# The first u spectra of an FFT convolution made ahead of and between the rounds of K's transform

## The chip, the cores and the metric

The kernel runs on one core of a Trainium2 chip. The metric is the device time of one launch in microseconds (us), the median of several runs. A core has TensorE (PE, with its weight loads shown apart as PEld), VectorE (DVE), ScalarE (ACT), GpSimd (POOL) and SyncE (SP), which here only issues DMAs. Each engine takes its own instructions in program order; semaphores order them against each other. TensorE writes to PSUM, which has eight banks of 2 KB per partition; SBUF holds everything else on the chip.

## The reference, cut to what matters

The block is an adaptive layer norm around a state space convolution (part A), and then around a spatial mixer with an MLP (part B). The change lies in part A.

```python
def _A_ref(u, A_re, A_im, B_re, B_im, C_re, C_im, log_dt, Dskip):
    ...
    P = jnp.exp(logdA[:, :, None] * l[None, None, :])
    K = jnp.einsum("dn,dnl,dn->dl", Cc, P, dB).real
    ...
    Kf = rfft2(Kp[:, None, :])
    Uf = rfft2(up[:, :, None, :])
    Yf = Uf * Kf[None, :, :, :]
    y = irfft2(Yf, s=(1, L2))[:, :, 0, :L]
    y = y.transpose(0, 2, 1) + u * Dskip[None, None, :]
    return y
...
h = _layernorm(x) * (1 + ca) + sa
x = x + ga * _A_ref(h, ...)
h = _layernorm(x) * (1 + cb) + sb
x = x + gb * _B_ref(h, ...)
```

u has 2048 rows of 512 channels, and N is 128. The convolution is made by products of transforms over 4096 points.

## The kernel before, in words

All of it is straight-line code, and the order of the instructions on every engine is that of the Python text (`manual_schedule`).

**The chunks** (L510 to L536). K is made in 32 chunks. Chunk k makes sines and cosines (`turns`), their products with exponentials on VectorE (`products`), and a burst of 64 matmuls into PSUM (`burst`, L485). A list `side[k]` adds to some chunks the normalising of u and u's first transform, whose results (`vs`) go out to the DRAM scratch VU (L437). The last of these stores belong to chunk 30. Each block of VU that is read later takes rows from all 64 columns that these stores write. Behind the chunks K gets its skip term (L536), and the first half of the table T2 is loaded (L538).

**K's first transform** (`k_first`, L559). Eight rounds r. A round issues 8 x 4 matmuls (L565; the chip runs each in two instructions, 64 a round) of 32 rows by 128 columns over 64 moving columns, into four PSUM banks, named by BANK as pk1, pk2, pz and py, each of which exists twice: eight banks. Then the four banks are copied to VK, two by ACT and two by DVE (L567 to L571; ACT's copies show as L118, the helper's line).

**The spectra loop** (L899). Sixteen steps, n = 0 to 15, one for each pair (jh, kc). `spectrum_u` (L589) makes u's spectrum of a step from a block of VU and T2, into pk1, and ACT copies it to us; `spectrum_k` (L612) makes K's from VK, T2 and T3 into both buffers of pk2; `multiply` (L623 to L628) is eight operations of DVE that read pk2 and us and write zc; `back` (L638) transforms zc of the step before into pz, ACT copies it to z, and POOL stores z to the DRAM scratch ZT (L641). Before the loop come the eight rounds and the u spectrum of step 0; step n makes the u spectrum of step n + 1. T2's second half (L915) is needed from kc = 4 on. In steps 11 to 13 the first inverse transforms (`inverse`, L663) are made from blocks of ZT.

**Loads.** SP issues them in the order of the text. Blocks of VU (`load_vu`, L578, two DMAs of 256 KB), of ZT (`load_inv`, L647) and raw weights (L676) share one pool, ldp, of seven buffers of 4 KB per partition. A load waits until its buffer's last reader is done, and SP's later loads queue behind it.

**After the loop** the remaining inverse transforms are made, and then part B runs: a mixer (`mix_w`) whose result goes through DRAM (GD), and the MLP (`chan`). A pool hv holds its windows: win, wh and wl, one buffer each.

## Time and profile before

| what | us |
|---|---|
| median of 3 runs | 823.54 (819.7 to 824.34) |
| the profiled execution | 824.95 |
| its span, first to last instruction | 823.2 |
| PE, PEld, DVE, ACT, POOL busy | 721.7, 547.0, 511.0, 339.1, 93.1 |
| chunks, about | 55 to 261 |
| `k_first` | 261.6 to 292.3 |
| spectra loop, to the last inverse transform in front of the mixer's load wait | 292.4 to 395.4 |
| the rest | 395.4 to 823.2 |

How to read it. A profile is of one execution. A timeline row gives start, length, engine, line, operation, out<-in, rows*columns of the array for a matmul, the shape, how many instructions are merged into the row, and in brackets how long the engine was idle before it and what released it. SPq is SP's queue of DMA issues. A line of grouped instructions ends with busy us, mean ns of one, and idle us in front of them by releaser. The row PEclk has one digit for each fortieth of the span: the TensorE clock granted, in tenths of full speed. "issue" is time in which an engine waited for nothing that the profile shows.

### The profile page before, as it was taken

Reading aid. Unit: us, or ns where it says so; the run is one execution under the profiler, and the core shown is the slowest. Engines: PE = TensorE matmul, PEld = TensorE weight load, DVE = VectorE, ACT = ScalarE, POOL = GpSimd, SP = SyncE. Lnnn points to the kernel's source line nnn. Section 1 sums busy time; section 2 is a strip of 40 time slices with the busy share of each in tenths; the row PEclk is TensorE's granted clock in tenths of the full one; section 3 lists DMA queues with packets and bytes.
Section 4 is the critical chain, followed back from the end, with each engine's and each line's share of the span. In section 5 each row is a group of like instructions: output and inputs, shape, how many; then the busy total and the mean of one; then the engine's idle time right before and its main releaser. Section 6 shows DMA issues by size and latency. Waiting matters only on the chain. (4 is left out here: it accounts for less than half of the span.)

```text
span 823.2 us, 17182 instructions
## 1 busy us (share of the span) xinstructions
PE 721.7 (88%) x7256; PEld 547.0 (66%) x7256; DVE 511.0 (62%) x883; ACT 339.1 (41%) x540; POOL 93.1 (11%) x186
## 2 busy tenths in 40 slices
PE   3597888988987989999549888999999999999994
PEld 1254455655556965665238887888888888888883
DVE  8779389988776347686479996644436261715211
ACT  3575467867674334454125553222213121221220
POOL 1011011111000000000126331010101010101000
PEclk9797788978788589999769899999999999999997
DMA  8231514242226999495703554110101010101011
GB/s 295 93 104 52 135 32 98 48 104 53 47 44 160 246 216 300 155 298 191 263 31 92 187 168 123 28 33 20 52 1 52 1 52 1 26 1 26 1 26 25
DMA packets 51045, 79.86 MB, mean 97 GB/s; under 512 B 5172, under 2 KB 37816, under 8 KB 49432
## 3 DMA queue, kind: packets, MB, share of 16 engines
q1 hardware_dynamic: 44808, 57.92, 25.9%
q0 software_dynamic: 6160, 20.85, 7.9%
q8 instruction: 57, 0.93, 0.5%
q14 instruction: 20, 0.16, 0.1%
HBM read 52.53 MB, written 26.21 MB: 96 GB/s over the span
## 5 line engine op out<-in xcount | busy, mean ns | idle before, releaser
L851 DVE TENSOR_TENSOR gl<-gf,gh 128x512 fp32r<-128x512 f32 (+1 forms) x48 | 30.4, 644 | 150.2 <-ACT gh L118 150.2
L118 ACT ACTIVATE gf<-pm 128x512 f32<-128x512 f32 (+1 forms) x48 | 27.0, 563 | 181.7 <-PE pm L845 178.1
L845 PE MATMUL pm<-nh,w3l 128*128 128x256 f32 (+1 forms) x352 | 98.5, 280 | 0.0
L844 PE MATMUL pm<-nl,w3h 128*128 128x256 f32 (+1 forms) x352 | 98.5, 280 | 0.0
L843 PE MATMUL pm<-nh,w3h 128*128 128x256 f32 (+1 forms) x352 | 98.4, 279 | 0.0
L856 PE MATMUL pa<-w4h,gh 128*128 128x512 f32 (+1 forms) x176 | 73.8, 419 | 3.2 <-ACT gh L118 0.9
L857 PE MATMUL pa<-w4l,gh 128*128 128x512 f32 (+1 forms) x176 | 69.3, 394 | 0.0
L843 PEld LDWEIGHTS pm<-nh,w3h 128*128 128x128 f32 (+1 forms) x352 | 65.4, 186 | 1.8
L845 PEld LDWEIGHTS pm<-nh,w3l 128*128 128x128 f32 (+1 forms) x352 | 65.5, 186 | 1.2
L844 PEld LDWEIGHTS pm<-nl,w3h 128*128 128x128 f32 (+1 forms) x352 | 65.2, 185 | 0.6
L858 PE MATMUL pa<-w4h,gl 128*128 128x512 f32 (+1 forms) x176 | 64.1, 395 | 0.0
L471 DVE SCALAR_TENSOR_TENSOR e<-sn,p 128x512 f32<-128x512 f32 x64 | 41.2, 685 | 26.1 <-PE kp L485 18.5
L451 PE MATMUL xx<-MG,ON 64*128 64x512 f32 x160 | 56.5, 454 | 0.0
L452 PE MATMUL xx<-MG,ON 64*128 64x512 f32 x160 | 56.5, 454 | 0.0
L118 ACT ACTIVATE sn<-xx 128x1024 f32<-128x1024 f32 x32 | 32.9, 1029 | 31.2 <-issue 17.7
L864 POOL DMA_DIRECT2D out<-KX x32 | 16.1, 508 | 257.1 <-DVE KX L862 257.1
L750 PE MATMUL pm<-nl,w1h 128*128 128x256 f32 x128 | 39.0, 305 | 6.8 <-DVE nl L721 6.8
L856 PEld LDWEIGHTS pa<-w4h,gh 128*128 128x128 f32 (+1 forms) x176 | 33.0, 188 | 17.8 <-ACT gh L118 13.2
L451 PEld LDWEIGHTS xx<-MG,ON 64*128 64x128 f32 x160 | 36.6, 228 | 7.7 <-issue 0.8
L485 PEld LDWEIGHTS kp<-e,e 128*32 128x32 f32 x2048 | 31.0, 112 | 15.6 <-issue 6.9
L473 DVE TENSOR_TENSOR e<-cs,p 128x1024 f32<-128x1024 f32 x32 | 39.0, 1218 | 1.5 <-ACT cs L118 1.5
L749 PE MATMUL pm<-nh,w1h 128*128 128x256 f32 x128 | 39.2, 306 | 0.0
(215 smaller groups left out, 1899.2 us busy)
## 6 DMA issues: line engine op xcount, KB each, us to landing
VU<-vs SPq DMA_DIRECT2D x64, 128.0 KB, 2.4
ld<-VU SPq DMA_DIRECT2D x32, 256.0 KB, 6.8
ZT<-z POOLq DMA_DIRECT2D x16, 512.0 KB, 4.2
ld<-ZT SPq DMA_DIRECT2D x16, 512.0 KB, 5.6
xu<-in_wm SPq DMA_DIRECT2D x6, 1024.0 KB, 9.9
wst<-in_w SPq DMA_DIRECT2D x18, 256.0 KB, 4.7
xu<-in_u SPq DMA_DIRECT2D x16, 256.0 KB, 4.2
KX<-in_u SPq DMA_DIRECT2D x16, 256.0 KB, 8.4
```

The lines of the kernel that those rows point to most:

```text
L118: return S.activation(out, in_, f, bias=bias, scale=scale)
L451: T.matmul(x[:, :512], la, ma, start=(i == 0), stop=(i == len(ops) - 1))
L452: T.matmul(x[:, 512:], lb, mb, start=(i == 0), stop=(i == len(ops) - 1))
L471: V.scalar_tensor_tensor(e0[:, 1, a], sn[:, 0], 1.0 - 2.0 * a, mg[:, a], op0=OP.mult, op1=OP.mult)
L473: V.tensor_mul(e0[:, 0], cs[:, 0:1].to_broadcast([128, 2, 512]), mg)
L749: T.matmul(p[:, e], W1h[:, k, c], hi[k], start=(k == 0), stop=False)
L843: T.matmul(p[:m, e], W3h[:, k, c], hi[k], start=(k == 0), stop=False)
L844: T.matmul(p[:m, e], W3h[:, k, c], lo[k], start=False, stop=False)
L845: T.matmul(p[:m, e], W3l[:, k, c], hi[k], start=False, stop=(k == 3))
L856: T.matmul(acc[i], gh[:m, e, s], W4h[:m, f], start=(f == 0), stop=False)
L857: T.matmul(acc[i], gh[:m, e, s], W4l[:m, f], start=False, stop=False)
L858: T.matmul(acc[i], gl[:m, e, s], W4h[:m, f], start=False, stop=(f == 10))
```

## The change

It does six things. T2's first half is loaded in chunk 25, and the blocks of u for steps 0, 1 and 2 in chunk 31, into a new pool lda of three buffers that lives from the chunks to the end. All blocks of VU now go through lda. The u spectrum of step 0 is made ahead of round 0, those of steps 1 and 2 behind rounds 1 and 4; step n (1 to 13) makes that of step n + 2, and us has three buffers. `k_first` no longer uses pk1: its rounds go in turn over pk2, pz and py, twice each, so six banks; DVE takes a third copy in rounds 1, 2, 4 and 5. ldp has four buffers, and some of the later loads (one ZT pair of each half, the second matrix's raw weights) go to lda. The pool hv is gone: the windows, wh and wl of part B take buffers of lda.

```diff
@@ -396,6 +396,7 @@
         V.tensor_mul(mods[0], mods[0], mods[2])
     pr.close()
 
+    lda = ctx.enter_context(pool("lda", bufs=3, side="right", reuse_waits="tile"))
     wk = a1.enter_context(pool("wk", bufs=2, reuse_waits="tile"))
     wk1 = a1.enter_context(pool("wk1", bufs=1, reuse_waits="tile"))
     uv = a1.enter_context(pool("uv", bufs=2, reuse_waits="tile"))
@@ -489,6 +490,15 @@
             g0 = (k // 2) * 8
             later.append(lambda: act(Kq[:, g0 // 64, g0 % 64:g0 % 64 + 8], kp))
 
+    vus = {}
+    steps = [(jh, kc) for jh in range(2) for kc in range(8)]
+
+    def load_vu(jh, kc):
+        t = vus[jh, kc] = lda.tile([128, 4, 256], F32, name="ld")
+        for ri in range(2):
+            Y.dma_start(t[ri * 64:ri * 64 + 64],
+                        dram(VU, jh * 1048576 + (ri * 32 + kc * 4) * 16384, [[256, 64], [16384, 4], [1, 256]]))
+
 
     side = {k: [] for k in range(40)}
     for n in range(3, 6):
@@ -505,6 +515,16 @@
             side[at(i) + 2].append(lambda i=i: u_dft(i - 1, 1))
         if i % 4 == 3 and i < 8:
             side[at(i) + 2].append(lambda i=i: load_u(i // 4 + 2))
+
+    T2 = []
+
+    def load_t2(i):
+        T2.append(up.tile([128, 16, 128], F32, name="xu"))
+        Y.dma_start(T2[i], A["T2"].rearrange("p (a b) -> p a b", a=32)[:, i * 16:i * 16 + 16])
+
+    side[25].append(lambda: load_t2(0))
+    for i in range(3):
+        side[31].append(lambda i=i: load_vu(*steps[i]))
 
     later = []
     with tc.manual_schedule():
@@ -534,9 +554,6 @@
         for f in later:
             f()
         V.tensor_add(Kq[:, :, :, 31], DS.rearrange("p (h g) -> p h g", h=2), Kq[:, :, :, 31])
-        T2 = [up.tile([128, 16, 128], F32, name="xu") for i in range(2)]
-        load_t2 = lambda i: Y.dma_start(T2[i], A["T2"].rearrange("p (a b) -> p a b", a=32)[:, i * 16:i * 16 + 16])
-        load_t2(0)
     a1.close()
 
 
@@ -548,16 +565,17 @@
     FI = c2.tile([128, 16, 2, 64], F32, name="FI")
     VK = [v0x.enter_context(pool("v0", side="right")).tile([128, 64, 2, 64], F32, name="VK0"),
           c2.tile([128, 64, 2, 64], F32, name="VK1")]
-    ldp = a2.enter_context(pool("ldp", bufs=7))
+    ldp = a2.enter_context(pool("ldp", bufs=4))
     s2x = ExitStack()
     s2 = s2x.enter_context(pool("s2", bufs=2))
     psy = a2.enter_context(pool("psy", bufs=2, space=PSUM, side="right"))
     psa = s2x.enter_context(pool("psa", bufs=2, space=PSUM))
-    BANK = ("pk1", "pk2", "pz", "py")
-    block = lambda: ldp.tile([128, 4, 256], F32, name="ld")
+    BANK = ("pk2", "pz", "py")
+    block = lambda pl: pl.tile([128, 4, 256], F32, name="ld")
 
     def k_first(r):
-        ps = [(psy if n == "py" else psa).tile([128, 8, 64], F32, name=n) for n in BANK]
+        ps = [(psy if n == "py" else psa).tile([128, 8, 64], F32, name=n)
+              for n in (BANK[(r * 4 + j) % 3] for j in range(4))]
         kv = KX.rearrange("p (g x) -> p g x", g=64)
         for gl in range(8):
             for j in range(4):
@@ -565,22 +583,16 @@
                 T.matmul(ps[j][:, gl], kv[rows, r * 8 + gl], FK[rows], start=True, stop=True)
         for j in range(4):
             o, i = VK[j // 2][:, :, j % 2, r * 8:r * 8 + 8], ps[j].rearrange("p g x -> p x g")
-            if j % 2:
+            if j % 2 or j == 2 and r in (1, 2, 4, 5):
                 V.tensor_copy(o, i)
             else:
                 act(o, i)
 
-    vus, zis, zcs = {}, {}, {}
-
-    def load_vu(jh, kc):
-        t = vus[jh, kc] = block()
-        for ri in range(2):
-            Y.dma_start(t[ri * 64:ri * 64 + 64],
-                        dram(VU, jh * 1048576 + (ri * 32 + kc * 4) * 16384, [[256, 64], [16384, 4], [1, 256]]))
+    zis, zcs = {}, {}
 
     def spectrum_u(jh, kc):
         vu = vus.pop((jh, kc))
-        us = s2.tile([128, 2, 3, 256], F32, name="us")
+        us = s2.tile([128, 2, 3, 256], F32, name="us", bufs=3)
         for i in range(2):
             q = psa.tile([128, 2, 256], F32, name="pk1")
             for ro in range(2):
@@ -641,7 +653,7 @@
         P.dma_start(ZT[jh][:, kc * 4:kc * 4 + 4], z)
 
     def load_inv(jh, g):
-        zz = [block() for h in range(2)]
+        zz = [block(lda if (jh, g) in ((0, 2), (1, 0)) else ldp) for h in range(2)]
         for h in range(2):
             c0 = 12 - 4 * g if h == 0 else 4 * g
             Y.dma_start(zz[h], dram(ZT[jh], (h * 16 + c0) * 32768, [[256, 128], [32768, 4], [1, 256]]))
@@ -683,8 +695,8 @@
             return split
         return hi, lo, load
 
-    def two(m, n):
-        return block().rearrange("p (a c) b -> p a (c b)", a=2)
+    def two(pl):
+        return lambda m, n: block(pl).rearrange("p (a c) b -> p a (c b)", a=2)
 
     def rstd(r, v):
         n = r.shape[-1]
@@ -756,7 +768,7 @@
         if g not in (0, 7):
             return
         if hf == 0:
-            win["pd"] = hv.tile([128, 4, 256], F32, name="win")
+            win["pd"] = block(lda)
         pd = win["pd"][:, hf * 2:hf * 2 + 2]
         gv = go.rearrange("p f (s c) -> p (f s) c", s=2)
         pv = pd.rearrange("p f (s c) -> p (f s) c", s=2)
@@ -773,14 +785,14 @@
     cn = {}
 
     def chan_load(g):
-        w = win[g] = hv.tile([128, 4, 256], F32, name="win")
+        w = win[g] = block(lda)
         for f, sh in enumerate((-1, 1, -2, 2)):
             Y.dma_start(w[:, f], dram(GD, f * 128 * 2560 + (2 + 2 * g + sh) * 128, [[2560, 128], [1, 256]]))
 
     def chan_split(g):
         w = win[g]
-        wh = hv.tile([128, 4, 256], F32R, name="wh")
-        wl = hv.tile([128, 4, 256], F32R, name="wl")
+        wh = lda.tile([128, 4, 256], F32R, name="ld")
+        wl = lda.tile([128, 4, 256], F32R, name="ld")
         act(wh, w)
         V.tensor_sub(wl, w, wh.bitcast(F32))
         win[g] = wh, wl
@@ -882,23 +894,21 @@
 
     seq = (7, 0, 1, 2, 3, 4, 5, 6)
 
-    steps = [(jh, kc) for jh in range(2) for kc in range(8)]
     with tc.manual_schedule():
         t3 = A["T3"].rearrange("p (a b) -> p a b", a=32)
-        load_vu(*steps[0])
         Y.dma_start(T3[:, :16], t3[:, :16])
         Y.dma_start(Gm, A["G"].rearrange("p (a b) -> p a b", a=2))
+        us = [spectrum_u(*steps[0])]
+        load_vu(*steps[3])
         for r in range(8):
             k_first(r)
-            if r == 3:
-                load_vu(*steps[1])
-            if r == 6:
-                load_vu(*steps[2])
-        us = spectrum_u(*steps[0])
+            if r in (1, 4):
+                us.append(spectrum_u(*steps[len(us)]))
+                load_vu(*steps[len(us) + 2])
         split = None
         for n, st in enumerate(steps):
             p = spectrum_k(*st)
-            multiply(*st, us, p)
+            multiply(*st, us[n], p)
             if n == 7:
                 v0x.close()
                 pw2 = ctx.enter_context(pool("pw2", side="right", reuse_waits="tile"))
@@ -907,10 +917,10 @@
                 W1h, W1l, ldw1 = weights(pw1, A["w1"], 512, 512, "w1", 4)
             if n > 0:
                 back(*steps[n - 1])
-            if n < 15:
-                us = spectrum_u(*steps[n + 1])
-            if n + 3 < 16:
-                load_vu(*steps[n + 3])
+            if 1 <= n < 14:
+                us.append(spectrum_u(*steps[n + 2]))
+            if 6 <= n + 5 < 16:
+                load_vu(*steps[n + 5])
             if n == 0:
                 load_t2(1)
             if n == 1:
@@ -923,7 +933,7 @@
                 split()
                 split = None
             if n in (8, 9, 14, 15):
-                split = (ldw1 if n < 10 else ldw2)(two, n % 2 * 2, 2)
+                split = (ldw1 if n < 10 else ldw2)(two(ldp if n < 10 else lda), n % 2 * 2, 2)
             if 9 <= n < 13:
                 load_inv(0, n - 9)
             if 11 <= n < 14:
@@ -933,7 +943,6 @@
         s2x.close()
         tp = lambda name, bufs=1, **k: pool(name, bufs, reuse_waits="tile", **k)
         cm = ctx.enter_context(tp("cm", 2, side="right"))
-        hv = ctx.enter_context(tp("hv", side="right"))
         gox = ExitStack()
         gop = gox.enter_context(tp("gop", 3, side="right"))
         psT = ctx.enter_context(tp("psT", space=PSUM))
```

## The prediction

> **What bounds the kernel now.** I read the page's engine shares first, then the windows view cut where the granted clock changes, then the timeline around K's first transform (`k_first`, L565).
>
> ```profile
> PE 721.7 (88%) x7256; PEld 547.0 (66%) x7256; DVE 511.0 (62%) x883; ACT 339.1 (41%) x540; POOL 93.1 (11%) x186
> ...
> PEclk9797788978788589999769899999999999999997
> ...
> 254.53:257.94 3.41, 2.48 (x72) 1.21 (x72) 3.38 (x6) 1.89 (x4) 0.00 (x0) 1.00 0.63 134
> 257.94:261.36 3.42, 1.10 (x64) 0.94 (x64) 1.57 (x3) 0.60 (x1) 0.00 (x0) 1.00 0.94 193
> 261.36:292.08 30.72, 28.13 (x512) 27.76 (x512) 0.50 1.05 258
> 292.08:295.49 3.41, 3.41 (x21) 1.92 (x18) 1.29 (x2) 2.02 (x5) 0.00 (x0) 0.50 1.03 233
> 295.49:387.60 92.11, 91.60 (x1428) 57.14 (x1424) 63.87 (x130) 43.98 (x125) 7.52 (x14) 1.00 0.78 239
> ```
>
> PE leads. A windows row gives start:end, length, busy time of PE, PEld, DVE, ACT, POOL (the 261.36 row, asked for L565 alone, gives PE and PEld), then clock, DMA share and GB/s. The spectra loop (295.49 to 387.60) is PE without a gap at full clock. The stretch before it is `k_first`: PE is just as busy, but the clock is 0.50 all through. That stretch is what the change touches.
>
> Why 0.50? In this trace the clock changes only at steps of 3.41 us. In such a step I count multiply-adds (rows x columns x moving columns x count) of the fp32 matmuls:
>
> ```profile
> L428 PE MATMUL pu<-xu,FU 32*64 32x512 f32 x8 | 1.6, 612 | 0.7 <-ACT vs L118 0.7
> L485 PE MATMUL kp<-e,e 128*32 128x64 f32 x64 | 1.1, 220 | 0.0
> ...
> 292.41 3.45 PE L589 MATMUL pk<-ld,xu 128*64 128x256 f32 x16
> 295.79 0.45 PE L612 MATMUL pk<-VK,xu 64*64 64x128 f32 x8
> ```
>
> The step from 254.53 holds 64 of L485 (16.8M) and 8 of L428 (8.4M), and the clock stays up. The next holds 64 of L485 alone, 16.8M, and it falls. A `k_first` step holds 64 matmuls of 32*128 x 64, again 16.8M: it stays down for nine steps. One u spectrum (L589, x16, 33.6M) fills the step from 292.08, and it rises. So the border lies between 16.8M and 25.2M a step. At full clock `k_first` without a pause would do up to twice its 16.8M and hold itself up.
>
> By the Trainium skill, "TensorE: Matmul & The Clock Gate", section "Part 1: The HAM clock gate", a window of about 3.4 us in which PE is busy raises the clock. The trace disagrees where it matters here: 28.13 us busy of 30.72, and 0.50.
>
> **The change: the end of the chunks.**
>
> ```profile
> 255.91 1.10 PE L485 MATMUL kp<-e,e 128*32 128x64 f32 x64
> ...
> 259.00 0.61 SPq L437 DMA_DIRECT2D VU<-vs  x1
> 259.31 1.10 PE L485 MATMUL kp<-e,e 128*32 128x64 f32 x64 [2.30 <-DVE e L474]
> 259.72 0.53 SPq L538 DMA_DIRECT2D xu<-in_T  x1
> ...
> 261.58 0.47 PE L565 MATMUL pk<-FK,KX 32*128 32x64 f32 x2 [1.17 <-DVE KX L536]
> ...
> 261.68 1.25 SPq L578 DMA_DIRECT2D ld<-VU  x2
> ...
> VU<-vs SPq DMA_DIRECT2D x64, 128.0 KB, 2.4
> ld<-VU SPq DMA_DIRECT2D x32, 256.0 KB, 6.8
> ...
> xu<-in_T SPq DMA_DIRECT2D x2, 1024.0 KB, 12.4
> ...
> DMA to landing us min/median/max: 3.4/6.8/13.1
> ```
>
> The first u spectrum (u0) is put on PE's queue ahead of `k_first`. Its block is read from VU, and each block takes from every column that the last store (issued 259.00, landing 2.4 us later) still writes. The load already leaves at 261.68, right after that landing; issuing it from chunk 31 cannot bring it forward. Its second half leaves some 0.6 us later and lands 3.4 (least) to 6.8 us (median) after: 265.7 to 269.1. I take 265.7, because T2's megabyte (259.72) no longer lies ahead of it. PE is done at 260.4, so it idles 5.3 us where it idled 1.17, and `k_first`, ready at 261.58, queues behind it. ACT's and DVE's evictions of `k_first` wait with it; SP has three loads, T3 and Gm to issue meanwhile.
>
> T2's first half moves six chunks ahead. It landed in 12.4 us; chunks are at least 3.4 us apart here (255.91 to 259.31), so it is there. Cost nothing.
>
> **The rounds.** Evictions of one round, and the nearest row for a PE that waits for a bank:
>
> ```profile
> 286.54 0.42 PE L565 MATMUL py<-FK,KX 32*128 32x64 f32 x1
> ...
> 286.77 0.69 DVE L569 COPY VK<-pk 128x512 f32<-128x512 f32 x1 [2.12 <-PE pk L565]
> ...
> 297.37 0.40 PE L612 MATMUL pk<-VK,xu 64*64 64x128 f32 x8
> ...
> 299.69 0.68 DVE L624 TENSOR_TENSOR mb<-pk,us 128x512 f32<-128x512 f32 x1
> ...
> 300.52 0.59 PE L612 MATMUL pk<-VK,xu 64*64 64x128 f32 x5 [0.51 <-DVE mb L624]
> ...
> 275.53 0.60 ACT L118 ACTIVATE VK<-pk 128x512 f32<-128x512 f32 x1 [2.33 <-PE py L565]
> 278.94 0.60 ACT L118 ACTIVATE VK<-pk 128x512 f32<-128x512 f32 x1 [2.33 <-PE py L565]
> ```
>
> A round takes 3.41 us (275.53 to 278.94). Four banks a round out of six instead of eight mean that the third and fourth bank of a round are the first and second of the round before. The second is evicted by DVE, which starts 0.23 us after the last matmul (286.54 to 286.77) and takes 0.69; PE goes on 0.15 us after such an end (300.37 to 300.52). That is 1.07 us after the last matmul, where the next would have come in 0.1 to 0.2: a stall of about 0.9 us at five borders (0-1, 2-3, 3-4, 5-6, 6-7), and one more before the first K spectrum, which u0 covered. After rounds 1 and 4 the inserted spectrum covers it; DVE takes a third eviction in rounds 1, 2, 4 and 5 while ACT copies us, and neither is on the path.
>
> The clock decides the rest. u0 runs at half clock, 3.4 us (292.41 to 295.79), with twice the work rate of `k_first`. Spread over two steps, it leaves at least one above the border in most positions, so the clock rises during u0 or round 0. What a round takes at full clock no row shows: between 3.41 (no gain) and half of it, 1.71. The nearest rows are a u spectrum and a weight load of 128 columns:
>
> ```profile
> 304.59 1.95 PE L589 MATMUL pk<-ld,xu 128*64 128x256 f32 x16
> 306.47 0.34 PE L612 MATMUL pk<-VK,xu 64*64 64x128 f32 x4
> ...
> L565 PEld LDWEIGHTS pk<-FK,KX 32*128 32x128 f32 x256 | 27.8, 327 | 4.1 <-issue 2.7 <-DVE KX L536 1.3
> ...
> L638 PEld LDWEIGHTS pz<-zc,Gm 64*128 64x128 f32 x128 | 11.1, 186 | 12.7 <-issue 9.6 <-ACT w2h L118 2.6 <-DVE w1l L682 0.5
> ```
>
> 1.88 us against 3.38, and 186 ns against 327: a factor of 1.8, so 1.8 us a round (taking these as clock 1.0 and 0.5).
>
> ```profile
> PE pk L565 <- issue: 2.4, 2, 1.8
> ```
>
> These two issue gaps in `k_first` (2.4 us in all) lie in the stretch with DMA share 1.05. Afterwards T2, x and four u blocks no longer crowd it; I keep 0.5.
>
> **The loop.** Step 0 no longer makes a spectrum. PE gains nothing: K's second spectrum (300.52) already waited for DVE with a u spectrum in front of it. What goes is cover; between 297.77 and 300.52 PE now idles 2.75 us, and a 3.41 us step with that hole has under 12M multiply-adds (33.6M in 1.9 us, for the 0.66 us left), so the clock falls once more: about 1.8 us. At step 14 the last u spectrum is gone:
>
> ```profile
> 383.91 1.95 PE L589 MATMUL pk<-ld,xu 128*64 128x256 f32 x16
> 385.78 0.45 PE L612 MATMUL pk<-VK,xu 64*64 64x128 f32 x8
> ...
> 383.97 0.68 DVE L624 TENSOR_TENSOR mb<-pk,us 128x512 f32<-128x512 f32 x1
> ```
>
> K's last spectrum then waits for mb (384.65 + 0.15) instead of starting at 385.78: 1.0 us gained.
>
> ```profile
> 304.69 1.09 ACT L118 ACTIVATE z<-pz 128x512 f32<-128x512 f32 x2 [4.07 <-PE pz L638]
> ...
> 310.40 1.09 ACT L118 ACTIVATE z<-pz 128x512 f32<-128x512 f32 x2 [2.86 <-PE pz L638]
> ...
> DMA to landing us min/median/max: 4.6/5.6/8.5
> ```
>
> Buffers: three blocks of u are always ahead, 17 us at 5.7 a step (304.69 to 310.40) against 13.1 us at most to land. The second block of inverse (0,2) is loaded one step later, 7.4 us before use, against 4.6 to 8.5 us of the ZT loads; 0 to 1.1 us, I take 0. SP queues T2's second half, T3's second half and the x loads behind the waits for u1 and u2; the first needed, T2, is used by the spectrum made in step 2, after three rounds and two and a half steps, some 22 us later, against 12.4 to land. POOL's queue is untouched. The windows of the later stage share the three blocks in the order the old pool gave them: 0.
>
> **The sum**, from the last chunk's end (260.41) to the first K spectrum. Before: 35.4 us (to 295.79). After: 5.3 wait, 3.4 u0, 2.6 round 0 (half of it at each clock), 7 x 1.8 = 12.6, 2 x 1.9 = 3.8, 6 x 0.9 = 5.4: 33.1. That is -2.3. To it: +1.7 for one relapse of the clock in rounds 2 to 7 (at 16.8M in 1.8 us a step with one stall of 0.9 has 23M, inside the border; with two it has 15M and falls), +1.8 in the loop's first steps, +0.5 issue, -1.0 at step 14. **+0.7 us** on the profiled execution's 824.95 (span 823.2), which is 1.4 above the median of 823.54. I say **825.5**.
>
> **Rivals.**
> A. The clock, once raised, holds through all rounds: no relapses, and stalls nearer 0.7. Then 825.5 - 3.5 - 1.2 = about 820.8, and 816.5 if u0 also finds the clock up and its load 2 us sooner (u0 and round 0 then save 2.3). For it: 25M held at 254.53. Against: steps with two stalls. By the Trainium skill's rule above, busy windows alone would keep the clock up, and it would be this case.
> B. Slower: the bank stalls keep `k_first` at half clock. Its place is the borders between rounds, its point a stall over about 1 us, where even a step with one stall drops below the border. With all eight rounds at 3.41 and all three spectra at 3.4, 5.3 + 27.3 + 10.2 + 5.4 = 48.2 against 35.4: +12.8, and with +1.8 and -1.0 it is 838; half of the rounds so, 832. For it: 16.8M a step never raised the clock. Against: each inserted spectrum raises it again. The Trainium skill, same page, section "A second HAM failure mode: psum-queue depth-cycling", tells of a clock that oscillates when PE idles briefly between groups; this trace has no such stall between rounds yet.
> C. The change does not do what it says, as u0 is not made at the end of the chunks but waits for a load at its median of 6.8 us: 3.4 us more, 829.
>
> **How the numbers follow.** Within 0.5% (about what a measurement of this kernel can tell) is 819.4 to 827.7. My forecast, one or two relapses, gives 821 to 830: chance 0.52 (0.05 faster, 0.37 same, 0.10 slower). A 0.18 (0.16, 0.02, 0), B 0.24 (0, 0.04, 0.20), C 0.06 (0, 0.03, 0.03). Together 0.21, 0.46, 0.33. The range reaches from A's low end to B's middle, 817 to 836; a round at full clock that gains nothing is B's end and stays outside.
>
> **What will show it.** The clock between 265 and 300: 0.5 to about 268, then 1.0 with one or two falls. PE idle about 5 us before L589's first matmul, released by the load of VU. L565 waiting for DVE or ACT about 0.9 us at five borders. L612's second group waiting 2.75 us for mb. The prediction is wrong if the clock stays at 0.50 through L565, if L589 starts before 264, or if L565 at clock 1.0 still takes over 3 us a round.

## The result and the profile after

The changed kernel takes 846.82 us (median of 4, 839.24 to 850.26) against 823.72 for the kernel before on the same chip (4 runs): a ratio of 1.0275, 95% interval 1.0227 to 1.0324. It is **slower**, by some 23 us, and above the forecast range of 817 to 836. The profiled execution has a span of 847.5 us against 823.2.

The page of the changed kernel, its engine shares and its rows for the clock and the DMA engines:

```profile
PE 729.7 (86%) x7256; PEld 550.3 (65%) x7256; DVE 513.6 (61%) x887; ACT 337.3 (40%) x536; POOL 93.2 (11%) x186
...
PEclk9797888977886569998967999999999999999997
DMA  8232522231337127997560546101011010101011
```

PE does the same 7256 instructions. Its busy time grows by 8 us, and the rest of the 24 is waiting. A slice is 21.2 us. In the DMA row the fourteenth and fifteenth (275 to 318 us) show 1 and 2, and behind them come 7, 9 and 9: `k_first` has become light in transfers and the loop full.

The windows of the changed kernel, cut where the granted clock changes (start:end, length, busy time of PE, PEld, DVE, ACT, POOL with counts, clock, DMA share, GB/s):

```profile
260.88:284.78 23.90, 15.78 (x175) 11.88 (x176) 3.24 (x6) 5.08 (x15) 0.00 (x0) 0.50 0.51 116
284.78:288.19 3.41, 2.95 (x97) 2.81 (x96) 1.73 (x3) 0.93 (x3) 0.00 (x0) 1.00 0.61 159
288.19:298.43 10.24, 9.99 (x130) 7.79 (x123) 3.33 (x6) 3.29 (x9) 0.00 (x0) 0.50 0.01 2
298.43:301.84 3.41, 2.95 (x97) 2.81 (x97) 1.76 (x3) 0.86 (x2) 0.00 (x0) 1.00 0.83 187
301.84:312.08 10.24, 9.42 (x159) 8.71 (x155) 2.70 (x5) 2.17 (x4) 0.00 (x0) 0.50 0.27 94
```

The clock is up for two single steps in the whole of `k_first` and falls again each time. The first K spectrum starts at 308.25 instead of 295.79.

The largest waits of PE in the changed kernel between 255 and 400 us (engine, line and tile, what it waited for: total us, times, longest):

```profile
PE pk L601 <- DMA ld<-VU: 8.9, 1, 8.9
PE pk L624 <- DVE mb L636: 8.4, 4, 5.5
PE kp L486 <- DVE e L475: 2.4, 1, 2.4
PE pk L601 <- issue: 1.4, 1, 1.4
PE py L583 <- ACT VK L118: 0.9, 2, 0.5
PE pk L583 <- ACT VK L118: 0.8, 3, 0.3
```

Before, no row of `k_first` had a wait for a load or for a bank. Now u0 (L601) waits 8.9 us for its block, the rounds (L583) wait for ACT's copies, and in the loop K's spectrum (L624) waits up to 5.5 us for DVE.

In the loop the same window of 57 us, first before, then changed:

```profile
330.00:387.00 57.00, 57.00 (x868) 35.30 (x864) 40.95 (x82) 27.52 (x78) 4.78 (x9) 1.00 0.72 227
```

```profile
330.00:387.00 57.00, 48.88 (x706) 30.21 (x706) 33.12 (x69) 24.33 (x68) 4.25 (x8) 0.94 1.06 291
```

PE was busy all of it and is now idle for 8 us, at a DMA share of 1.06 instead of 0.72. `k_first` shows the reverse. SP's timeline in the kernel before has the loads in `k_first`:

```profile
271.16 0.33 SPq L538 DMA_DIRECT2D xu<-in_T  x1
...
273.59 0.40 SPq L917 DMA_DIRECT2D T<-in_T  x1
...
277.62 7.50 SPq L652 DMA_DIRECT2D KX<-in_u  x4
```

In the changed kernel SP's queue says why (the rows with the most waiting, 255 to 400 us), and its timeline, when the late loads leave:

```profile
SPq L499 <- PE pk L601: 70.8, 13, 22.6
SPq L659 <- PE pk L601: 11.9, 2, 7.1
```

```profile
297.75 1.23 SPq L499 DMA_DIRECT2D ld<-VU  x2
299.02 0.60 SPq L523 DMA_DIRECT2D xu<-in_T  x1
322.30 1.24 SPq L499 DMA_DIRECT2D ld<-VU  x2
323.58 1.64 SPq L927 DMA_DIRECT2D T<-in_T  x1
328.00 1.39 SPq L499 DMA_DIRECT2D ld<-VU  x2
329.43 2.17 SPq L664 DMA_DIRECT2D KX<-in_u  x4
```

A block of u (L499) needs a buffer of a ring of three, so SP waits for a u spectrum, up to 22.6 us at a time. T2's second half (L523) leaves only at 299.02 (271.16 before), T3's at 323.58 (273.59 before), x from 329.43 on (277.62 before). They meet the loop's own transfers there. The changed kernel's timeline shows what that does at PE's longest wait in the loop:

```profile
378.62 1.15 ACT L118 ACTIVATE w1h<-ld 128x512 fp32r<-128x512 f32 x2 [6.93 <-DMA ld<-in_w]
379.28 1.29 DVE L694 TENSOR_TENSOR w1l<-ld,w1h 128x512 fp32r<-128x512 f32 x2 [8.45 <-ACT w1h L118]
...
381.92 0.66 PE L624 MATMUL pk<-VK,xu 64*64 64x128 f32 x2 [5.51 <-DVE mb L636]
```

Raw weights land late, ACT waits 6.93 us for them, DVE 8.45 us for ACT, and PE 5.51 us for the product (mb) that stands behind w1l on DVE. What the profile calls a release by DVE goes back to a DMA.

The 24.3 us of the two spans by stage:

| stage | predicted | measured |
|---|---|---|
| end of the chunks (260.41, now 259.83) | 0 | -0.6 |
| from there to the first K spectrum (35.4, now 48.4) | -0.1 with relapse and issue | +13.0 |
| first to third K spectrum (10.7, now 13.9) | +1.8 | +3.3 |
| third K spectrum to the last of `back` (87.0, now 97.5) | -1.0 | +10.5 |
| after it (429.7, now 427.8) | 0 | -1.9 |

### The profile page after: what moved, and what is told of

The parts are those of the page before. It is cut to its first block, busy times and chain, and to the rows that moved or that the text cites. A ratio compares the mean times of both kernels' runs of the same rounds, so it can differ in the third digit from the quotient of the medians.

```text
span 847.5 us, 17159 instructions
## 1 busy us (share of the span) xinstructions
PE 729.7 (86%) x7256; PEld 550.3 (65%) x7256; DVE 513.6 (61%) x887; ACT 337.3 (40%) x536; POOL 93.2 (11%) x186
## 4 chain that ended last, share of the span: by engine, by line
PE 32%; DVE 8%; ACT 6%; issue 2%; DMA 1%; POOL 1%; DVEq 0%; POOLq 0%; SPq 0%
PE pa L868 6%; PE pa L870 5%; PE pa L869 5%; PE pm L857 3%; PE pm L855 3%; PE pm L856 3%; ACT gh L118 3%; ACT gf L118 2%; DVE st L708 2%; PE pT L725 1%; DVE h L713 1%; PE ph L813 1%; PE ph L812 1%; PE ph L814 1%; DVE h L712 1%
## 5 line engine op out<-in xcount | busy, mean ns | idle before, releaser
L624 PE MATMUL pk<-VK,xu 64*64 64x128 f32 x768 | 38.4, 298 | 10.1 <-DVE mb L636 8.9
L601 PE MATMUL pk<-ld,xu 128*64 128x256 f32 x256 | 36.6, 433 | 10.3 <-DMA ld<-VU 8.9
L624 PEld LDWEIGHTS pk<-VK,xu 64*64 64x64 f32 x768 | 33.1, 147 | 16.8 <-issue 16.0
```

What stands on the lines that cost most here:

```text
L624: T.matmul(p[gh][kk * 64:kk * 64 + 64, i, ro], w, VK[jh][rows, ri * 32 + k1].rearrange("p j g -> p (j g)"), start=(ri == 0), stop=(ri == 1 ...
```

## The experiments

Three causes were open: the low clock with its bank waits, u0's wait for its block, and SP's order with the crowded loop. "To K" below is the time from the chunks' end to the first K spectrum, "loop" that from there to the last `back`, both of the profiled execution: 35.4 and 97.7 before, 48.4 and 111.4 as changed. Ratios are to the kernel before.

**Eight banks (e1)**. The changed kernel with one edit:

```diff
-    BANK = ("pk2", "pz", "py")
+    BANK = ("pk1", "pk2", "pz", "py")
...
-              for n in (BANK[(r * 4 + j) % 3] for j in range(4))]
+              for n in BANK]
```

> The changed kernel with eight banks in K's first transform again (pk1, pk2, pz and py, one of each a round); all else stays as changed. Theory 1 (the clock follows the array work of each 3.41 us step, with the border near 0.72 of a full-clock step of dense work, and the waits for banks of 0.46 to 0.62 us a round keep the steps below it): u0, split over two steps, still does not raise the clock; u1 does, at about 281.4, and the rounds behind it hold it without stalls, so the first K spectrum starts near 295 instead of 308.25 and the whole is 830 to 835. Rival 1 (the stalls matter only by their own length, six of about 0.5): 308.25 - 3 = 305, and 843 to 844. Rival 2 (with eight banks the clock oscillates just the same, as K's first transform never holds it): 845 to 848.

Measured 832.77 us (825.76 to 843.22, 4 runs), ratio 1.0156 (1.0082 to 1.0231): theory 1's number, 10 us above the kernel before instead of 23. The window of all eight rounds with u1 and u2 in this run, and PE's waits up to the loop:

```profile
263.51:283.43 19.92, 19.57 (x546) 17.25 (x544) 11.35 (x19) 10.35 (x26) 0.00 (x0) 1.00 0.44 128
```

```profile
PE pk L601 <- DMA ld<-VU: 8.2, 1, 8.2
PE pk L583 <- ACT us L118: 0.3, 2, 0.2
```

Eight rounds and two u spectra in 19.92 us at clock 1.00; less 3.9 for the spectra (1.95 each) that is 2.0 us a round. Without bank waits `k_first` holds the clock by itself. In this execution u0 itself raised it (at 263.01, not at u1 as expected): its chunks ended at 252.11, and u0 lay otherwise to the clock's steps. So the size depends on the phase, the holding does not. This execution is the fastest of the four and the only one with a trace, so how much of the median's gain is the holding alone is not shown. Its loop stayed at 109.9 us: the crowding is another matter.

**SP's order (e2, e12).** First (e2) the loads were given to POOL's queue:

```diff
-            Y.dma_start(X2[...
+            P.dma_start(X2[...
...
         load_vu(*steps[3])
+        load_t2(1)
+        P.dma_start(T3[:, 16:], t3[:, 16:])
+        P.dma_start(FI, ...)
```

(T2's second half goes to POOL's queue as well, x behind rounds 1, 3, 5 and 7; the old places in the loop are taken out.)

> The changed kernel with the second halves of T2 and T3, FI and the x loads issued from POOL's queue (T2, T3 and FI right behind u0, x behind rounds 1, 3, 5 and 7) instead of from SP behind its waits for u spectra; all else as changed. Theory 1 (the loop lost 10.5 us because SP, held by a ring of three blocks, issues some 4 MB during the loop that it issued before during K's first transform, and the loop's raw weights and K spectra come late): first K spectrum at 308 +- 1 as in the changed kernel, the loop from the third K spectrum to the last back transform 88 to 90 us instead of 97.4, DMA share in the loop near 0.8 instead of 1.06, the whole 836 to 839. Rival 1 (the loop is longer for the clock and for the u spectra made two steps ahead, not for its transfers): 845 to 848. Rival 2 (the transfers moved into K's first transform slow its instruction fetch): first K spectrum 2 to 4 us later, the whole 839 to 843.

Measured 842.86 us (841.49 to 847.31), ratio 1.0246 (1.0204 to 1.0288). To K 53.5, loop 102.7: the loop gained 8.7 us and the start lost 5. POOL's and PE's timelines of that run show the loss:

```profile
256.47 0.60 POOL L523 DMA_DIRECT2D xu<-in_T  x1 [26.88 <-DMA VU<-vs]
261.78 0.53 POOL L904 DMA_DIRECT2D T<-in_T  x1 [4.71 <-DVE KX L556]
262.30 0.53 POOL L905 DMA_DIRECT2D FI<-in_FI  x1
...
274.30 1.98 PE L601 MATMUL pk<-ld,xu 128*64 128x256 f32 x8 [13.94 <-DMA ld<-VU]
```

Nothing on POOL waits for u0, so 2.5 MB went out in front of its block. SP sent the block at 264.83 instead of 262.06, as the last stores of VU landed later too, and PE waited 13.94 us. By the Trainium skill, "DMA: Bandwidth & Descriptors", section "Issuing engines are not separate DMA queues", another issuing engine gives no other DMA engines; the trace agrees, with DMA share 1.01 from 260 to 274 us.

So the test was made again on SP (e12), with the start left as changed:

```diff
         us = [spectrum_u(*steps[0])]
+        load_t2(1)
+        Y.dma_start(T3[:, 16:], t3[:, 16:])
+        Y.dma_start(FI, ...)
         load_vu(*steps[3])
...
                 us.append(spectrum_u(*steps[len(us)]))
+                load_x(len(us) - 2)
                 load_vu(*steps[len(us) + 2])
+        load_x(2)
```

(x's last load moves to step 2; the old places in the loop are taken out.)

> The changed kernel with nothing altered but the order of SP's loads: T2's and T3's second halves and FI ahead of the first load that waits for a u spectrum, three x loads behind rounds 1, 4 and 7, the fourth in step 2. Six banks and the start as changed. Theory 1 (of the 24 us, the 10 of the loop come from the 5 MB that SP, waiting for u spectra, sends in the loop): first K spectrum at 308 +- 1.5 as changed, its loop 100 to 104 us instead of 111.45, the whole 836 to 840. Rival (the loop is longer for the u spectra two steps ahead or the low clock at its head alone): loop 108 us or more, 843 to 848.

Measured 833.45 us (830.49 to 838.38), ratio 1.0140 (1.0112 to 1.0168): 12 us above the kernel before instead of 23. The part of this run's loop that lies 34 to 91 us behind the first K spectrum, as the window of the kernel before does, and PE's waits in its loop:

```profile
336.00:393.00 57.00, 55.95 (x826) 34.67 (x826) 40.10 (x81) 27.32 (x76) 4.79 (x9) 1.00 0.85 241
```

```profile
PE pk L624 <- DVE mb L636: 3.6, 5, 1.5
PE pz L650 <- ACT w2h L118: 1.8, 1, 1.8
```

The DMA share is 0.85 (0.72 before, and 0.95 in the changed kernel at the same distance behind its first K spectrum), the longest wait for mb 1.5 instead of 5.5 us, and the loop takes 102.0 instead of 111.4. The order of SP's loads cost 9.5 of the loop's 13.7 us. The first K spectrum also came at 302.02, outside the expected 306.5 to 309.5: u0 began 0.5 us sooner in its clock step than in the changed kernel and raised the clock at 270.49. With one trace of each, that part of the gain can't be put down to the order of the loads.

**The ring alone (e3)**, in the kernel before:

```diff
-    ldp = a2.enter_context(pool("ldp", bufs=7))
+    ldp = a2.enter_context(pool("ldp", bufs=4))
...
-        t = vus[jh, kc] = block()
+        t = vus[jh, kc] = block(lda)
```

> The kernel before with nothing of the change but the split of the buffers: blocks of VU in a ring of three (lda), four buffers in ldp, and part B's windows in lda. K's first transform keeps eight banks and no inserted spectrum. Theory 1 (the ring of three holds SP back, and with it T2's and T3's second halves, x and FI, which then crowd the loop): first K spectrum at 295 to 297 as before, the loop 6 to 11 us longer than its 86.95 from the third K spectrum to the last back transform, the whole 830 to 834. Rival (the ring costs nothing, and the loop's loss belongs to the late clock and to the spectra made two steps ahead): 823 to 825.

Measured 827.64 us (820.24 to 831.27, 10 runs), ratio 1.0048 (1.0016 to 1.0079). To K 32.1, loop 102.4; its DMA share from 330 to 387 us is 0.98. The loop loses 4.7 us, less than the 6 to 11 expected. The stretch before it gains 3.3: its DMA share is 0.43 (262 to 293 us) instead of 1.05, and the two issue gaps of 2.4 us that the kernel before had there are gone. Here SP sends T3's second half 5 us behind the first K spectrum and FI 44, in the changed kernel 15 and 52 us behind it, so the loads crowd it less. The direction is theory 1's, the size not.

**u0's block first (e5)**. T3's first half and Gm behind round 1:

```diff
-        Y.dma_start(T3[:, :16], t3[:, :16])
-        Y.dma_start(Gm, ...)
         us = [spectrum_u(*steps[0])]
...
                 load_vu(*steps[len(us) + 2])
+            if r == 1:
+                Y.dma_start(T3[:, :16], t3[:, :16])
+                Y.dma_start(Gm, ...)
```

> The changed kernel with T3's first half and Gm loaded behind the u spectrum of step 1 instead of ahead of the blocks of u on SP; all else as changed. Theory 1 (u0 started at 268.75 because T3 and Gm stood in front of its block): u0 starts near 265.5, still split over two clock steps so that it does not raise the clock, and everything behind it comes some 3 us sooner: first K spectrum at 304 to 306, the whole 842 to 845. Rival 1 (the block is bound by VU's last store and its own latency): u0 at 268 or later, 846 to 848. Rival 2 (3 us sooner puts u0 inside one step and the clock rises there): first K spectrum at 298 or sooner, below 840.

Measured 845.24 us (840.63 to 848.81), ratio 1.0270 (1.0238 to 1.0302). SP in the changed kernel, then SP in this run and PE's wait for the block:

```profile
261.01 0.36 SPq L899 DMA_DIRECT2D T<-in_T  x1
261.42 0.42 SPq L900 DMA_DIRECT2D Gm<-in_G  x1
262.06 1.92 SPq L499 DMA_DIRECT2D ld<-VU  x3
```

```profile
262.20 3.89 SPq L499 DMA_DIRECT2D ld<-VU  x6
```

```profile
PE pk L601 <- DMA ld<-VU: 6.1, 1, 6.1
```

PE waits 6.1 us instead of 8.9, so 2.8 us less; To K is 45.6. The chunks end at 261.03 here (259.83 in the changed kernel), so the block leaves 1.2 us behind them instead of 2.2. From the issue of its second half (262.84, and 262.72) to u0 it takes 4.3 us instead of 6.0. So of the 2.8 us with T3 and Gm in front, about 1 is the block's later issue and 1.8 its slower landing. u0 still did not raise the clock. The time moved by 1.6 us, inside the scatter of single runs, so this cause is seen in the trace only.

**u0 inside `k_first` of the kernel before (e4)**. To see the clock without the other parts:

```diff
+    side[25].append(lambda: load_t2(0))
...
             k_first(r)
+            if r == 1:
+                us = spectrum_u(*steps[0])
...
-        us = spectrum_u(*steps[0])
```

> The kernel before (eight banks, seven buffers, all blocks of VU as before) with two edits: T2's first half is loaded in chunk 25, and the u spectrum of step 0 is made between rounds 1 and 2 instead of behind round 7. Theory 1 (one dense u spectrum inside a step raises the clock, and K's first transform without waits for banks does enough array work at full clock to hold it): clock 1.00 from about 271.6, rounds 2 to 7 in 1.8 us each instead of 3.41, first K spectrum at 283 to 286 instead of 295.79, the whole 811 to 818. Rival 1 (K's first transform is held by its transfers and instruction fetch at a DMA share of 1.05, not by the clock): the rounds stay above 3 us, 821 to 824. Rival 2 (the clock rises and falls back within two steps): one or two rounds gain, 819 to 822.

Measured 822.06 us (814.57 to 825.52, 10 runs), ratio 1.0017 (0.9978 to 1.0057): no change, a miss for theory 1's 811 to 818. Windows of this run, and PE's waits in them:

```profile
261.43:271.67 10.24, 10.17 (x144) 8.63 (x144) 2.59 (x5) 3.11 (x7) 0.00 (x0) 0.50 0.79 196
271.67:281.91 10.24, 7.81 (x265) 7.40 (x261) 3.87 (x6) 4.19 (x9) 0.00 (x0) 1.00 1.07 273
281.91:292.15 10.24, 7.28 (x135) 6.90 (x129) 3.19 (x6) 3.00 (x6) 0.00 (x0) 0.50 1.08 250
```

```profile
PE pk L570 <- issue: 4.8, 2, 2.4
```

The clock rose at 271.67, as expected, and until 278.3 PE did the rounds at full rate. Then it stood for 2.4 us with nothing in the profile to wait for, the clock fell, and it stood so once more. In the packets of the DMA engines a 16 KB instruction fetch starts at 277.95 and one at 286.35, and PE stands from 278.29 and from 286.78. It goes on 1.4 us after each of them is in (279.29 and 287.65). In e4, e6 and e7 the first gap stands at the same instruction of the program, and the second 128 matmuls and 128 weight loads further on. The two issue gaps of the kernel before (0.5 and 1.8 us, at clock 0.50) lie as far apart. With the clock up PE uses its instructions faster (a round in 2.0 us instead of 3.41), and here the two fetches came 8.4 us apart at a DMA share of 1.07.

**Less in that stretch (e6, e7, e8).** Two runs with the same edit and fewer transfers there: x by POOL behind the stores of ZT (e6),

```diff
+            if 1 <= n < 9:
+                load_x((n - 1) // 2, ((n - 1) % 2 * 2, (n - 1) % 2 * 2 + 1))
```

> As the run with u0 between rounds 1 and 2 of the kernel before, and the x loads (4 MB) taken out of K's first transform: issued by POOL behind the stores of ZT in steps 1 to 8, two of 256 KB a step. Theory 1 (that run's gain was given back by instruction fetches of PE, 16 KB each, that come late while the DMA share is over 1: two gaps of 2.4 us, each taking the clock down for two or three steps): with 2 MB less in that stretch the gaps become fewer or shorter, first K spectrum at 285 to 290 instead of 292.44, the whole 815 to 820. Rival 1 (5.6 MB in 24 us still fill the queues): the gaps stay, 820 to 823. Rival 2 (the loop pays for the x loads): first K spectrum sooner, the loop 102 us or more instead of 99.2, 820 to 824.

and blocks of u in a ring of three of their own, four other buffers, and SP's loads in a new order (e7):

```diff
+            if r == 1:
+                for i in range(1, 3):
+                    load_vu(*steps[i])
+                us = spectrum_u(*steps[0])
+                load_vu(*steps[3])
+                load_t2(1)
+                Y.dma_start(T3[:, 16:], t3[:, 16:])
+                Y.dma_start(FI, ...)
...
+            if n + 4 < 16:
+                load_vu(*steps[n + 4])
+            if n in (1, 3, 5, 11):
+                load_x((1, 3, 5, 11).index(n))
```

> As the run with u0 between rounds 1 and 2 of the kernel before, with SP's loads paced: blocks of u in a ring of three of their own (four other buffers), so that SP, waiting for u0 and later for each u spectrum, sends 2 MB ahead of u0, then one block, T2's and T3's second halves and FI, and the x loads in steps 1, 3, 5 and 11. Theory 1 (late instruction fetches under a full DMA share, not the array, ended the fast clock): no or one issue gap in K's first transform, clock 1.00 from about 271.7 through the loop, rounds of 2.0 us, first K spectrum at 284 to 287, loop 98 to 102 us, the whole 812 to 819. Rival 1 (the bytes not sent before the loop crowd it as in the changed kernel): loop 105 us or more, 820 to 826. Rival 2 (the clock falls again without a gap): first K spectrum at 289 or later.

The first: 823.76 us (817.72 to 827.14), ratio 1.0011 (0.9986 to 1.0035), issue gaps of 5.1 us, To K 33.5, loop 100.7: rival 1, the gaps stay. The second: 823.35 us (818.90 to 824.68), ratio 1.0001 (0.9980 to 1.0021), To K 28.8, loop 104.5: the gaps halved to 2.5 us, and what was gained went back in the loop. The same with u0 behind round 0 (e8):

```diff
-            if r == 1:
+            if r == 0:
```

> The same as the paced run, with u0 behind round 0 instead of round 1. Theory 1 (the clock rises only after a step with more than about 0.72 of a full-clock step of dense work): u0 runs from about 265.5 to 269, split between the steps that end at 268.3 and 271.7; the first then holds about 0.75, at the border, so the clock rises at 268.3 in some executions and not until u1 in the others. Where it rises: first K spectrum at 283 to 285, the whole 811 to 817; where it does not: 292 to 296, 820 to 826. Rival (any burst of dense work raises the clock at the next step): it rises at 268.3 each time, 811 to 817.

Measured 825.72 us (818.51 to 831.03), ratio 1.0028 (0.9998 to 1.0058). The two outcomes that theory 1 told of are not seen apart in twelve times, and 811 to 817 was never reached; nothing is built on this run.

**Loads spread (e9)**. The paced run with 2 MB behind u0, x's fourth load and FI behind round 7, x in steps 2, 4 and 7, the first inverse transforms a step later:

```diff
+            if r == 7:
+                load_x(3)
...
+            if r == 7:
+                Y.dma_start(FI, ...)
...
+            if n in (2, 4, 7):
+                load_x((2, 4, 7).index(n))
...
-            if 11 <= n < 14:
-                inverse(0, n - 11)
+            if 12 <= n < 15:
+                inverse(0, n - 12)
```

> As the paced run, with the loads spread: behind u0 only one block of u, T2's second half and T3's second half (2 MB), the fourth x load and FI behind round 7, the other x loads in steps 2, 4 and 7; the first inverse transforms one step later (steps 12 to 14), as their blocks of ZT came late in the paced run. Theory 1 (the stretch from the chunks to the end of the loop has slack in its transfers only when they are spread, and PE's clock is held by array work alone): no issue gap over 1 us in K's first transform, clock 1.00 from 271.7 on, first K spectrum at 284 to 287, loop 98 to 101 us, the whole 812 to 817. Rival 1 (what the fast clock saves before the loop is given back in it whatever the order, as it was in the runs with 33.5 + 100.7, 32.1 + 99.2 and 28.8 + 104.5 us): 821 to 824. Rival 2 (the clock falls at the end of its third step without a gap, as it did near 282 in three runs): first K spectrum at 289 to 292.

Measured 819.19 us (812.76 to 822.47), ratio 0.9953 (0.9927 to 0.9978). Windows of this run and PE's wait in `k_first`:

```profile
260.77:271.01 10.24, 10.13 (x144) 8.63 (x144) 2.63 (x5) 3.11 (x7) 0.00 (x0) 0.50 0.82 209
271.01:284.67 13.66, 12.53 (x417) 11.90 (x417) 7.73 (x12) 7.45 (x15) 0.00 (x0) 1.00 0.56 184
```

```profile
PE pk L571 <- issue: 0.2, 1, 0.2
```

With no gap the clock holds for four steps, to the end of `k_first`; To K is 24.2 us instead of 35.4. The loop took 103.2. The waits from 330 to 358 us:

```profile
DVE w1l L688 <- ACT w1h L118: 5.0, 1, 5.0
...
ACT w1h L118 <- DMA ld<-in_w: 4.2, 2, 3.5
...
PE pk L618 <- DVE mb L630: 2.9, 2, 2.1
```

PE's wait goes back over DVE and ACT to the raw weights, which SP sent (336.81) behind x's load of step 7 (331.28 to 333.21) and a block of u. Hence x in steps 0, 2 and 5 (e11):

```diff
-            if n in (2, 4, 7):
-                load_x((2, 4, 7).index(n))
+            if n in (0, 2, 5):
+                load_x((0, 2, 5).index(n))
```

> As the spread run, with its other three x loads in steps 0, 2 and 5 instead of 2, 4 and 7. Theory 1 (the spread run lost some 5 us in its loop because the x load of step 7 stood ahead of w1's raw blocks on SP, whose copies hold up ACT and DVE and with them K's spectrum near 349): no wait over 1 us near step 8, first K spectrum at 284 to 287 as there, loop 97.5 to 100.5 instead of 103.2, the whole 811 to 816. Rival (the loop is full of transfers whatever their order): loop 102 to 104, 818 to 821.

Measured **816.89 us** (815.92 to 819.28), ratio 0.9938 (0.9916 to 0.9959): 0.6% faster than the kernel before, clear of its interval, and a little above the 811 to 816 expected. The wait near step 8 is gone and the loop is 100.6 us. In this execution a gap of 2.4 us stood in `k_first` again, with an instruction fetch beginning at 281.91, though the DMA share was 0.30 in the 2.9 us before it. What makes a fetch start late is not settled.

**The change mended (e10)**: eight banks, blocks of u first, u1 right behind u0, u2 behind round 5, T2 and the others ahead of the waits.

```diff
+        us = [spectrum_u(*steps[0])]
+        us.append(spectrum_u(*steps[1]))
+        load_vu(*steps[3])
+        load_vu(*steps[4])
         Y.dma_start(T3[:, :16], t3[:, :16])
         Y.dma_start(Gm, ...)
-        us = [spectrum_u(*steps[0])]
-        load_vu(*steps[3])
+        load_t2(1)
...
```

(The banks change as in e1, u2 moves behind round 5, and the other loads go where e9 has them.)

> The changed kernel with its three losses mended: eight banks in K's first transform, the blocks of u ahead of T3 and Gm on SP, and T2's and T3's second halves, FI and one x load ahead of the waits for later spectra. The u spectrum of step 1 is made right behind that of step 0, so that some clock step is full of dense work; that of step 2 behind round 5. Theory 1 (the three causes add up: start wait and low clock 13.0 us, loop's head 3.3, crowding 10.5): u0 near 266, clock 1.00 from 271 at the latest, first K spectrum at 288 to 292, loop 98 to 103 us, the whole 815 to 824, so the loss of 24 us is gone. Rival (something else in the change costs, such as the u spectra two steps ahead): the loop stays at 108 us or more and the whole at 828 or more.

Measured 830.54 us (828.52 to 833.79), ratio 1.0100 (1.0072 to 1.0129). 16 of the 23 us are gone, not all. u0 began at 266.13 and the clock rose as forecast, but fell at 281.60, behind a step in which PE paused for 0.57 us (278.65 to 279.22, an issue gap), so the first K spectrum came at 296.51; the loop took 103.3, with waits for mb of 6.0 us in five. The rival's 828 or more came true, its loop of 108 did not. What of the loop's 6 us beyond the 97.7 is the spectra two steps ahead was not tried.

## Why the prediction was wrong

- **"The clock decides the rest" was right, its border misplaced.** The quantity was right: array work in a step of 3.41 us. But the first part left the border between 16.8M and 25.2M multiply-adds, and the sum then took a step with one bank wait at 23M to be "inside the border". The 23M came true: the two fast steps of the changed kernel have 23.6M and 23.3M by the rows that start in them (90 and 89 of L583 at 0.262M). Behind both the clock fell. The step of 254.53 in the kernel before, which held, has 24.1M when counted so. One wait a step is enough, and the relapse came each time, not once.

  How good the count is: from about 250 to 395 us the fourteen traces have 573 steps with fp32 matmuls alone or with none. Behind none of the 126 steps under 23M was the clock 1.00, and behind none of the 415 above 25.5M was it 0.50. The 32 between went either way, and as a trace can lack some rows, the border can't be placed closer. This holds for fp32 alone: earlier, where the chunks' sines and cosines are made from tiles of another type (fp32r), steps with 33.6M in all stay at 0.50 (179.44 in the kernel before). What the expectations call 0.72 of a full-clock step is 0.72 of the 33.6M that dense fp32 work does in a step at half clock.
- **"u0 raises the clock" failed.** The text said that spread over two steps it leaves one above the border "in most positions". u0 ran from 268.75 to 272.3 over a step that began at 267.71: 2.4 us of dense work, 23M, in one step, and 1.2 us with a half-rate round, some 21M, in the next. The first is at the border at most, the second is under it, and the clock stayed down. Of the six traces in which u0 stands ahead of the rounds it raised the clock in three (e1, e2, e12) and not in three (the changed kernel, e5, e10). In e12 it began half a microsecond sooner in its step than in the changed kernel, so how u0 fell on the clock's steps was in part luck.
- **The bank wait was over-sized.** 0.9 us was forecast. The changed kernel's timeline at the border of rounds 0 and 1:

```profile
276.05 0.42 PE L583 MATMUL py<-FK,KX 32*128 32x64 f32 x1
276.72 0.47 PE L583 MATMUL pk<-FK,KX 32*128 32x64 f32 x1 [0.25 <-ACT VK L118]
```

  That is 0.67 us from start to start, 0.46 beyond the usual 0.2 at half clock. Its own length hardly matters: five of them and 0.6 us ahead of the first K spectrum add up to some 3 us, and without them e1 is 10 us above the kernel before instead of 23.
- **u0's start**: 265.7 forecast, 268.75 measured, a wait of 8.9 us instead of 5.3. The last store's landing was right as the first release. Two things failed. SP has T3 and Gm to issue "meanwhile", but they went ahead of the block (261.01 against 262.06). And the block was given the least landing time of 3.4 us, as if nothing lay ahead of it, and took 6.0 from the issue of its second half. e5 gives 2.8 us for T3 and Gm.
- **The loads that SP queues behind the waits for u1 and u2, put at no cost, were a miss of 10.5 us.** The question asked was whether each load lands in time; 22 us against 12.4 held. The one not asked was what these loads collide with. The profile before had the answer: `k_first` at DMA share 1.05 and the loop at 0.78 in the rows quoted there. Making the first lighter was counted as a gain (0.5 us of issue gaps left of 2.4), and the loop that the loads moved to was not looked at. In e12 SP's order alone gives back 9.5 us of the loop.
- **The loop's head**: +1.8 forecast, +3.3 measured; the hole for mb was there, but the clock was low from 301.84 to 312.08 already, and fell once more behind the hole. The 1.0 us of step 14 can't be read out of the crowded loop.
- **Rival B** had 48.2 us for the stretch to the first K spectrum, and 48.4 came. Its mechanism was right, its point was not: it asked for a wait over 1 us, and 0.46 to 0.6 did it. Its sum also reached 48 with six waits of 0.9 and a start wait of 5.3, where shorter waits, two fast steps and a start wait of 8.9 stood. Its whole was 838, since it too had 0 for the loop.
- **The Trainium skill's rule** of busy windows ("TensorE: Matmul & The Clock Gate", section "Part 1: The HAM clock gate") fails again: from 288.19 to 298.43 PE is busy for 9.99 of 10.24 us at 0.50. The Trainium skill, same page, section "A second HAM failure mode: psum-queue depth-cycling", tells of a clock that goes up and down as PE idles briefly between groups; the trace agrees, with two rises and two falls in `k_first`.

## What to carry to other kernels

When a buffer ring makes the issuing engine wait, list every load behind it, in bytes, and add them to the DMA share of the stage where they will now run: landing in time is not enough if that stage is already at 0.8. Where PE is busy at half clock, count its array work per clock step: a phase that is light at half clock can hold the full clock if one dense burst raises it and nothing interrupts it, so a short wait a round can cost as much as the whole phase gains. A wait for DVE or ACT that appears in a stage with a DMA share over 1 should be followed back to the load.

## What was not expected of the hardware

- PE's instruction fetches (16 KB each) show as gaps in `k_first`, and where a trace has two, 128 matmuls and 128 weight loads apart. They take 0.5 to 4.7 us (e4, e6, e7, e10, e11), and behind them the clock stayed down for three steps or more in e4, e6 and e7. At half clock the kernel before has 0.5 and 1.8 us of them, and e3, with a DMA share of 0.43 there, none.
- The phase of the clock's steps to the work decides some microseconds: the chunks ended at 252.11 in one execution and between 259.2 and 261.5 in the others, and the kernel before alone ran from 813.47 to 825.54 us in 19 runs on one chip.
- In the changed kernel T3 and Gm stand ahead of the u blocks on SP although the text has the blocks in chunk 31, so on SP the order is not that of the text everywhere; why was not settled.
